# Block-sparse attention and a squared-ReLU MLP on one core: two transposes, one score block and a weight block change places, and the fixed key blocks change slots

## The chip, the cores and the metric

The kernel runs on one core of a Trainium2 chip. Times are device microseconds (us) from one launch. The engines are PE (matmul), ACT, DVE and POOL (elementwise), and SP, which here only issues DMAs; each works through its own queue in order and waits on semaphores of the others.

## The reference

Four batches, eight heads, 768 positions, head size 64; all in float32. Attention is masked by blocks of 32 positions: a query block sees the first and the last key block (the fixed blocks), its own and its two neighbours (the window), and three blocks drawn at random; the first and the last query block see everything. Behind it stands an MLP.

```python
mask = np.abs(blk_i - blk_j) <= window
mask = mask | (blk_i == 0) | (blk_j == 0) | (blk_i == n_blocks - 1) | (blk_j == n_blocks - 1)
for qb in range(n_blocks):
    for kb in sampled_blocks[qb]:
        mask[qb * block:(qb + 1) * block, kb * block:(kb + 1) * block] = True
scores = np.where(mask, scores, -1000000000.0)
...
attn = attn / (np.sum(attn, axis=-1, keepdims=True) + 1e-09)
return np.matmul(attn, v).astype(np.float32)
...
h = np.maximum(x @ w_in, 0.0)        # x: 3072 x 512, w_in: 512 x 2048
return (h * h @ w_out).astype(np.float32)
```

## The kernel before

**Tiles and slots.** The work is cut into 24 tiles of 128 query rows (six per batch), and each tile into two halves of four heads. A query block of 32 rows has eight key slots of 32: in `KG` (keys) and in `V` (values; slots 0 to 3 are the partition quarters of `VA`, slots 4 to 7 those of `VB`). Slots 0 and 1 hold the fixed blocks, 2 to 4 the random ones, 5 to 7 the window. For the first three tiles, which have a `V` each (`V[0]`, `V[1]`, `V[2]`), the fixed blocks of the values come by one small DMA into one query block's place of `V[0]` (`load_static`), and are copied from there to the other places (`copy_static`, L215: `V[0]` and `V[1]` on ACT, `V[2]` on POOL). The random blocks come by one DMA each from SP (`load_sampled`, L339).

**A half's steps** (class `Half`, L379): scores `s` on PE (L427), maxima `m` on DVE (L439), exponentials `p` on ACT (L481), transposes `pt` on PE (L496), copies `pT` (L506 ACT, L508 DVE), values `pv` on PE (L536), normalization into `x` on DVE (L552 to L567). The first and the last query block of a batch go through the class `Whole` (`g`, `pg`, `ptg`, `pvg`).

**The MLP** takes three tiles at a time (a chunk c). `turn` (L902) transposes the three x on PE into PSUM banks `xt`, splits them on ACT into a high part `xh` and on DVE into the rest `xl`; `hidden` (L922) makes 12 matmuls `ph` of 128 hidden columns f, then `r` and `gp` on ACT; `project` (L952) adds into three output banks `po`. For chunk 0, `project` takes `gp` and a plain `WO[f]`, six rows in the trace of PE for its three float32 matmuls.

**The weights** come as 64-bit words `craw` by DMA from POOL. `cut_next` (L863) takes one block of `cuts` at a time through its stages: load, then three calls later two operations on ACT (L833, L835), one call later two on DVE (L844, L845). `cuts` begins with `PRE` blocks of w_in (part 0), then takes a block of w_out (part 1) and one or more of w_in in turn.

```python
    cuts = [(f, 0) for f in range(PRE)]
    for f in range(NF):
        cuts.append((f, 1))
```

So the order before is w_in 0, 1, 2, 3, w_out 0, 1, w_in 4, and so on; the fourth block's ACT operations stand just ahead of the first `xh`. `W` are the cut blocks of w_in, `WO` those of w_out; `wi` is a block of w_in split in two (L889 ACT, L892 POOL).

**What sets the order.** Each engine's queue is in the order in which the code calls it. The first stage steps a `Stream` of the first three tiles' units until they are done (L1061); at counts of `now` it calls `copy_static` and `cut_next` in between. Then chunk 0 of the MLP runs, and after each yielded group of matmuls the stream of the next tiles is stepped once. PSUM tiles named `s`, `pt`, `xt` and `ph` share five banks that go round; a new one waits for the readers of the fifth before it.

Of the kernel before, what the change touches and what calls it, by code (L numbers as in the profile page):

```python
# [23 lines left out]
BLK = 32  # L24
NBLK = S // BLK
NRAND = 3
# [25 lines left out]
LEAD = 2  # L52
PRE = 4
AHEAD = 3
# [20 lines left out]
CUT_0 = (43, 5)  # L75
LOAD_0 = 36
MORE = 1
KEYS_GAP = 4
CUT_1 = 3

FIXED_0 = (7, 14, 24)
LATE = (0, 4)
# [14 lines left out]
def tile_block_sparse_attention_moe(ctx: ExitStack, tc, kd, knd, qd, qgd, vd, vnd, samp, wcat, out):  # L97
# [108 lines left out]
    def load_static(k, u, eng=nc.sync):  # L206
        us = halves(k, u)
        if us is None:
            return
        n = 1 if k == 0 else NJ  # L210
        src = columns(vd[order[k][0], V_STATIC * BLK :], us)
        src = src.unsqueeze(1).broadcast_to([2 * BLK, n, src.shape[-1]])
        eng.dma_start(places(values_of(k)[0], slice(0, 2 * BLK), slice(0, n), us), src)

    def copy_static(k, i, copy):  # L215

        us = slice(i, i + 1)
        src = places(V[0][0], slice(0, 2 * BLK), slice(0, 1), us)
        dst = places(V[k][0], slice(0, 2 * BLK), slice(1 if k == 0 else 0, NJ), us)
        copy(dst, src.broadcast_to(list(dst.shape)))  # L220
# [45 lines left out]
    def copy_keys(b, t, window=nc.gpsimd.tensor_copy):  # L266
# [3 lines left out]
        for us in (slice(0, 1), slice(1, 2)) if t == 0 else (slice(0, 2),):  # L270
# [21 lines left out]
    def load_kg(b, t):  # L292
# [3 lines left out]
        for j in sorted(groups(t)):  # L296
            for r in range(NRAND):
                nc.sync.dma_start(
                    kg[:, j, 2 + r].rearrange("p b c -> p (b c)").unsqueeze(1), k4[:, bass.ds(vals[NRAND * j + r], 1), :]
                )  # L300
        if t < 2:
            for i in range(2):
                src = k4[:, i * (NBLK - 1)].unsqueeze(1)
                dst = kg[:, :, i].rearrange("p j b c -> p j (b c)")
                nc.sync.dma_start(dst, src.broadcast_to(list(dst.shape)))
# [6 lines left out]
    def static_keys(b, t, u, copy):  # L312

        src = st["kn", b, u][:, 0 : NBLK : NBLK - 1].rearrange("p i a c -> p i (a c)").unsqueeze(1)
        dst = st["kg", b, t][:, :, 0:2, 2 * u : 2 * u + 2].rearrange("p j i a c -> p j i (a c)")
        copy(dst, src.broadcast_to(list(dst.shape)))
# [22 lines left out]
    def load_sampled(k, u, eng, on, midway=None):  # L339
# [7 lines left out]
        for j in sorted(groups(t)):  # L347
            if midway and j == NJ // 2:
                load_window(*midway)
            for r in range(NRAND):  # L350
                at = slice(0, BLK) if r == 2 else slice((2 + r) * BLK, (3 + r) * BLK)
                dst = places(VB if r == 2 else VA, at, slice(j, j + 1), us)
                eng.dma_start(dst, v4[:, bass.ds(vals[NRAND * j + r], 1)])  # L353
# [541 lines left out]
    def split_wo(c, f):  # L895
# [4 lines left out]
        wo[c, f] = split(c, WO[f], f"wo{c}_{f}")  # L900

    def turn(c):  # L902

        xh = pool["x"].tile([P, NCC, TOK], F32R, tag="xh", name=f"xh{c}", bufs=1)
        xl = pool["x"].tile([P, NCC, TOK], F32R, tag="xl", name=f"xl{c}", bufs=1)
        for i in range(UC):
            if c * UC >= MOVED:
# [3 lines left out]
            else:  # L911
                x = X.pop(order[c * UC + i])
                pt = bank(f"xt{c}_{i}")
                for cc in range(NCC):
                    nc.tensor.transpose(pt[:, cc * P : (cc + 1) * P], x[:, cc * P : (cc + 1) * P], ident)
            p3 = pt.rearrange("p (c q) -> p c q", c=NCC)
# [109 lines left out]
    warm = one.tile([P, 1], F32, name="warm")  # L1026
    nc.scalar.activation(warm, negative, AF.Exp)
    st["idx"] = indices()
    start = tc.tile_pool(name="start", bufs=1)
    begin = start.__enter__()  # L1030
    for k in range(1, UC):
        V[k] = [begin.tile([P, NJ, 2, HW // 2], F32, name=f"V{k}{c}") for c in range(2)]
    load_static(0, 0)
    load_q(0, 0)
    load_vn(0, 0, nc.gpsimd)
# [6 lines left out]
    load_window(2, 1)  # L1042
    load_sampled(2, 1, nc.sync, SP)
    first = copy_keys(0, 0)
    for _ in groups(0):
        next(first)
    load_vn(0, 1, nc.gpsimd, begin)
    deque(first, 0)
    deque(copy_keys(0, 1), 0)
    deque(copy_keys(0, 2), 0)  # L1050
    cut_next()
    for i in range(2):
        copy_static(2, i, nc.gpsimd.tensor_copy)
    cut_next()
    fixed = [(FIXED_0[k] + i, k, i) for k in range(2) for i in range(2)]
    side = lambda name: ps_o.tile([P, 512], F32, tag="o", name=name)
# [4 lines left out]
    while work.todo or work.running:  # L1061
# [4 lines left out]
        if fixed and now >= fixed[0][0]:  # L1066
            copy_static(*fixed.pop(0)[1:], nc.scalar.copy)
        if now == LOAD_0:
            cut_next()
        if now >= CUT_0[0] and (now - CUT_0[0]) % CUT_0[1] == 0:  # L1070
            cut_next()
# [12 lines left out]
    for c in range(NCH + 1):  # L1084
        work.drain(c, now)
        for _ in moe(c):
# [6 lines left out]
            if c == 0 and now % CUT_1 == 0 and done < len(cuts) + AHEAD + 2:  # L1093
                cut_next()
# [68 lines left out]
```

## Time and profile before

| | |
|---|---|
| timed runs | 730.67, 734.06, 734.63 us; median 734.06 |
| profiled execution | 729.79 us, its span on the core 727.8 us |
| busy, share of the span | PE 705.2 us (97%), DVE 520.6 (72%), POOL 507.6 (70%), ACT 500.0 (69%) |
| mean granted clock of PE | 0.997 |
| chain of work that ended last | PE 90%, DMA 5%, DVE 2% |
| HBM traffic | 100.54 MB read, 6.29 MB written |

PE, DVE, ACT and POOL shares are means over the whole span. The kernel has a first stage of some 48 us, attention alone, and then a long one in which the MLP's matmuls and the next tiles' attention are interleaved on PE. The timed runs are 0.9 to 4.8 us longer than the profiled one.

### The profile page before, as it was taken

Reading aid. Unit: us, or ns where it says so; the run is one execution under the profiler, and the core shown is the slowest. Engines: PE = TensorE matmul, PEld = TensorE weight load, DVE = VectorE, ACT = ScalarE, POOL = GpSimd, SP = SyncE. Lnnn points to the kernel's source line nnn. Section 1 sums busy time; section 2 is a strip of 40 time slices with the busy share of each in tenths; the row PEclk is TensorE's granted clock in tenths of the full one; section 3 lists DMA queues with packets and bytes.
Section 4 is the critical chain, followed back from the end, with each engine's and each line's share of the span. In section 5 each row is a group of like instructions: output and inputs, shape, how many; then the busy total and the mean of one; then the engine's idle time right before and its main releaser. Section 6 shows DMA issues by size and latency. Waiting matters only on the chain.

```text
span 727.8 us, 21584 instructions
## 1 busy us (share of the span) xinstructions
PE 705.2 (97%) x7648; PEld 572.7 (79%) x7648; DVE 520.6 (72%) x1016; ACT 500.0 (69%) x1114; POOL 507.6 (70%) x612
## 2 busy tenths in 40 slices
PE   5878999999999999999999999999999999999997
PEld 2665666668888888878888888887888888889896
DVE  6887777768787777678886876768887676645442
ACT  5678777888866875688877776578877777533222
POOL 6956583238875776768777586667877577769884
PEclk9999999999999999999999999999999999999999
DMA  9987979654535547846445456666455352101001
GB/s 286 243 298 225 323 245 270 172 173 114 146 99 135 167 120 205 203 120 192 119 125 136 113 156 181 178 163 182 136 144 146 106 156 48 36 1 43 1 1 43
DMA packets 96699, 108.25 MB, mean 149 GB/s; under 512 B 13825, under 2 KB 82178, under 8 KB 96594
## 3 DMA queue, kind: packets, MB, share of 16 engines
q1 hardware_dynamic: 90114, 82.51, 41.8%
q0 software_dynamic: 5904, 23.06, 9.6%
q8 instruction: 61, 1.00, 0.6%
q10 hardware_dynamic: 576, 1.31, 0.5%
q14 instruction: 44, 0.36, 0.2%
HBM read 100.54 MB, written 6.29 MB: 147 GB/s over the span
## 4 chain that ended last, share of the span: by engine, by line
PE 90%; DMA 5%; DVE 2%; SPq 1%; ACT 1%; issue 1%; ACTq 0%
PE ph L929 37%; PE po L969 32%; PE po L958 6%; PE s L427 6%; PE pv L521 5%; DMA V<-in_v_dram 3%; PE pv L718 1%; DMA q<-in_q_dram 1%; PE g L641 1%; PE pv L536 1%; SPq L353 1%; PE pt L496 1%; DVE xl L919 1%; ACT xh L918 0%; DVE mg L656 0%
## 5 line engine op out<-in xcount | busy, mean ns | idle before, releaser
L467 ACT ACTIVATE pm<-p 32x256 f32<-32x256 f32 x528 | 219.2, 415 | 23.9 <-DVE p L450 16.3
L929 PE MATMUL ph<-xh,wi 128*128 128x384 f32 x960 | 201.3, 347 | 1.1 <-DVE wi L891 1.1
L929 PEld LDWEIGHTS ph<-xh,wi 128*128 128x128 f32 x960 | 170.6, 188 | 25.0 <-issue 11.3
L892 POOL TENSOR_TENSOR wo<-WO,wo 128x512 fp32r<-128x512 f32 x112 | 144.5, 1290 | 52.1 <-DVE wo L891 51.6
L933 ACT ACTIVATE r<-ph 128x384 f32<-128x384 f32 x128 | 62.8, 491 | 166.4 <-PE ph L929 166.0
L969 PE MATMUL po<-wo,gh 128*128 128x512 f32 x672 | 175.3, 396 | 0.0
L948 POOL TENSOR_TENSOR gl<-gf,gh 128x384 fp32r<-128x384 f32 x112 | 113.7, 1015 | 72.5 <-DVE gf L945 63.4
L945 DVE SCALAR_TENSOR_TENSOR gf<-ph,r 128x384 f32<-128x384 f32 x112 | 61.9, 553 | 124.0 <-ACT r L933 124.0
L969 PEld LDWEIGHTS po<-wo,gh 128*128 128x128 f32 x672 | 123.9, 188 | 26.0 <-issue 4.5
L929 PE MATMUL ph<-xl,wi 128*128 128x384 f32 x480 | 104.0, 338 | 0.0
L892 POOL TENSOR_TENSOR wi<-W,wi 128x512 fp32r<-128x512 f32 x56 | 72.5, 1294 | 38.2 <-DVE wi L891 18.2
L969 PE MATMUL po<-wo,gl 128*128 128x512 f32 x336 | 98.7, 402 | 0.0
L892 POOL TENSOR_TENSOR wi<-W1B,wi 128x512 fp32r<-128x512 f32 x64 | 83.3, 1301 | 20.1 <-ACT wi L889 17.3
L929 PEld LDWEIGHTS ph<-xl,wi 128*128 128x128 f32 x480 | 85.3, 188 | 0.1
L969 PEld LDWEIGHTS po<-wo,gl 128*128 128x128 f32 x336 | 62.1, 189 | 21.5 <-issue 4.3
L891 DVE TENSOR_REDUCE wo<-WO 128x512 fp32r<-128x512 f32 x112 | 74.9, 669 | 0.0
L439 DVE TENSOR_REDUCE m<-s 128x2 f32<-128x512 f32 (+1 forms) x96 | 61.7, 683 | 8.1 <-PE s L427 7.7
L940 ACT ACTIVATE gh<-r 128x384 fp32r<-128x384 f32 x112 | 58.9, 526 | 9.5 <-ACT r L933 0.4
L427 PE MATMUL s<-KG,q 64*32 64x256 f32 x1344 | 50.1, 382 | 0.0
L958 PE MATMUL po<-WO,gp 128*128 128x512 f32 x96 | 46.5, 620 | 2.7 <-DVE WO L845 2.7
L450 DVE TENSOR_TENSOR p<-s,m 128x512 f32<-128x512 f32 (+1 forms) x72 | 46.1, 681 | 0.3
L473 DVE STREAM_TRANSPOSE pT<-pm 128x1024 f32<-128x1024 f32 (+1 forms) x36 | 41.3, 1146 | 0.3 <-ACT pm L467 0.3
(115 smaller groups left out, 804.7 us busy)
## 6 DMA issues: line engine op xcount, KB each, us to landing
craw<-in_w_dram POOLq DMA_DIRECT2D x32, 512.0 KB, 5.8
V<-in_v_dram SPq DMA_DIRECT2D x462, 32.5 KB, 2.6
KG<-in_k_dram SPq DMA_DIRECT2D x189, 64.0 KB, 1.9
V<-in_v_dram SPq DMA_DIRECT2D x26, 390.0 KB, 6.4
KG<-in_k_dram SPq DMA_DIRECT2D x12, 768.0 KB, 6.1
q<-in_q_dram SPq DMA_DIRECT2D x24, 256.0 KB, 3.4
out_dram<-ot SPq DMA_DIRECT2D x22, 256.0 KB, 5.3
V<-in_v_dram SPq DMA_DIRECT2D x14, 292.5 KB, 6.2
```

The costliest lines, as they stand in the source:

```text
L427: nc.tensor.matmul(self.sb[e][g * BLK : (g + 1) * BLK, i * NSLOT : (i + 1) * NSLOT], q[r, j, pr, :], kg[r, j, :, pr, :], start=True, stop= ...
L439: nc.vector.tensor_reduce(m[at, e], self.sb[e][at].rearrange("p (i c) -> p i c", i=2), axis=AX, op=ALU.max)
L467: nc.scalar.activation(p[a * BLK : (a + 1) * BLK, g], x[g * BLK : (g + 1) * BLK, :, a], AF.Exp, scale=SCALE)
L891: nc.vector.tensor_reduce(w[:, 0], src.unsqueeze(2), axis=AX, op=ALU.max)
L892: nc.gpsimd.tensor_tensor(w[:, 1], src, w[:, 0], op=ALU.subtract)
L929: nc.tensor.matmul(ph[:, :TOK], w, x, start=(i == 0), stop=(i == len(steps) - 1))
L933: nc.scalar.activation(r, ph[:, :TOK], AF.Relu)
L940: nc.scalar.activation(gh, r, AF.Square)
L945: nc.vector.scalar_tensor_tensor(gf, ph[:, :TOK], 0.0, r, op0=ALU.max, op1=ALU.mult)
L948: nc.gpsimd.tensor_tensor(gl, gf, gh, op=ALU.subtract)
L958: nc.tensor.matmul(acc[c][u], g[:, u * P : (u + 1) * P], WO[f], start=(f == 0), stop=(f == NF - 1))
L969: nc.tensor.matmul(acc[c][u], g[:, at], w[:, k], start=first, stop=(f == NF - 1 and g is gl))
```

## The change

It does five things.

1. The first two x of chunk 0 are transposed at count 55 of the first stage, ahead of the last `pv` (`TURN_0`, `turn_x`); the third where all three were.
2. `work.step(0)` is called before `turn`, so the fourth tile's scores `s_3_0` stand ahead of the third x.
3. `PRE` is 3: the order of weight blocks becomes w_in 0, 1, 2, w_out 0, w_in 3, w_out 1, w_in 4.
4. The fixed blocks go to slots 1 and 2, the random ones to 0, 3 and 4, for keys and values. `copy_static` copies all 128 partitions for `V[1]` and `V[2]` (the outer slots are written over by the random blocks' DMAs afterwards; DVE clears them once with two memsets, so that what is copied is defined), and one slot of 32 partitions at a time for `V[0]`.
5. `V[1]`'s copies move to the start of ACT's queue, `V[2]`'s copies on POOL from behind the third tile's keys to behind the first half of the first tile's, and the loads of `V[2]`'s random blocks behind them in the code.

```diff
-PRE = 4
+PRE = 3
...
+TURN_0 = 55
...
+FIXED = 1
+RAND = (0, 3, 4)
+
 CUT_1 = 3
-
-FIXED_0 = (7, 14, 24)
+CUT_AT = 0
+
+FIXED_0 = (7, 20)
...
-    def copy_static(k, i, copy):
+    def copy_static(k, i, copy, n=None):
 
         us = slice(i, i + 1)
-        src = places(V[0][0], slice(0, 2 * BLK), slice(0, 1), us)
-        dst = places(V[k][0], slice(0, 2 * BLK), slice(1 if k == 0 else 0, NJ), us)
+        rows = slice(0, P) if n is None else slice((FIXED + n) * BLK, (FIXED + n + 1) * BLK)
+        src = places(V[0][0], rows, slice(0, 1), us)
+        dst = places(V[k][0], rows, slice(1 if k == 0 else 0, NJ), us)
         copy(dst, src.broadcast_to(list(dst.shape)))
...
+    turned_x = {}
+
+    def turn_x(c, i):
+        x = X.pop(order[c * UC + i])
+        pt = bank(f"xt{c}_{i}")
+        for cc in range(NCC):
+            nc.tensor.transpose(pt[:, cc * P : (cc + 1) * P], x[:, cc * P : (cc + 1) * P], ident)
+        return pt
+
     def turn(c):
...
+        first = turned_x if c == 0 else {}
...
-                x = X.pop(order[c * UC + i])
-                pt = bank(f"xt{c}_{i}")
-                for cc in range(NCC):
-                    nc.tensor.transpose(pt[:, cc * P : (cc + 1) * P], x[:, cc * P : (cc + 1) * P], ident)
+                pt = first[i] if i in first else turn_x(c, i)
...
+    for place in (0, NJ - 1):
+        nc.vector.memset(V[0][0][place * BLK : (place + 1) * BLK, 0], 0.0)
     st["idx"] = indices()
...
     load_static(0, 0)
+    for i in range(2):
+        copy_static(1, i, nc.scalar.copy)
...
-    load_sampled(2, 1, nc.sync, SP)
     first = copy_keys(0, 0)
     for _ in groups(0):
         next(first)
     load_vn(0, 1, nc.gpsimd, begin)
+    for i in range(2):
+        copy_static(2, i, nc.gpsimd.tensor_copy)
+    load_sampled(2, 1, nc.sync, SP)
...
-    for i in range(2):
-        copy_static(2, i, nc.gpsimd.tensor_copy)
...
+        if now == TURN_0:
+            turned_x.update({i: turn_x(0, i) for i in range(UC - 1)})
...
+    work.step(0)
     load_vn(1, 0, nc.gpsimd)
```

**Engine PE, end of the first stage.** The queue before, from the last matmuls of the third tile's second half (`pv_2_1`) to the first `ph` and the fourth tile's scores:

```order
L536 MATMUL pv_2_1_1109<-V_125,pT_2_1_1106 32x65 x4
L915 MATMUL xt_0_1177<-ident,x_0_482 128x128 x4
L915 MATMUL xt_1_1184<-ident,x_1_953 128x128 x4
L915 MATMUL xt_2_1191<-ident,x_2_1101 128x128 x4
L929 MATMUL ph_0_1201<-xh_1175,WI 128x384 x4
L427 MATMUL s_3_0_0_1206<-KG_89,q_3_627 32x256
```

The queue of the change, in two pieces (between them stand six more rows of `pv_2_1` and fourteen of `s_3_0`):

```order
L502 MATMUL pt_2_1_1_1087<-ident,p_2_1_1033 128x128 x4
L914 MATMUL xt_0_1113<-ident,x_0_486 128x128 x4
L914 MATMUL xt_1_1118<-ident,x_1_957 128x128 x4
L542 MATMUL pv_2_1_1123<-V_126,pT_2_1_1110 32x65 x4
L542 MATMUL pv_2_1_1123<-V_127,pT_2_1_1110 32x65 x4
```

```order
L433 MATMUL s_3_0_0_1184<-KG_89,q_3_631 32x256
L433 MATMUL s_3_0_1_1185<-KG_89,q_3_631 32x256
L914 MATMUL xt_2_1213<-ident,x_2_1105 128x128 x4
L942 MATMUL ph_0_1223<-xh_1207,WI 128x384 x8
L942 MATMUL ph_0_1223<-xl_1208,WI 128x384 x4
L942 MATMUL ph_1_1260<-xh_1207,wi_1_1220 128x384 x8
```

`xt_0` and `xt_1` now stand ahead of `pv_2_1`; all of `s_3_0`, 16 rows here and 32 matmuls in the trace, stands ahead of `xt_2` and no longer inside `ph_0`.

**Engine ACT, the turn and the first two hidden blocks.** Before, from the fourth weight block's cut (`W_83` is w_in 3) to the second `r`:

```order
L833 ACTIVATE W_83<-craw_0_951 128x512
L835 ACTIVATE craw_0_951<-craw_0_951,below 128x512
L918 CAST xh_1175<-xt_0_1177 128x4x128
...
L936 ACTIVATE gp_0_1239<-r_0_1237 128x384
L833 ACTIVATE WO_91<-craw_1_1036 128x512
L835 ACTIVATE craw_1_1036<-craw_1_1036,below 128x512
L889 CAST wi_2_1247<-W_82 128x512
...
L481 ACTIVATE p_3_0_1231<-s_3_0_0_1206,m_3_0_1228 128x256 x2
L481 ACTIVATE p_3_0_1231<-s_3_0_1_1207,m_3_0_1228 128x256 x2
L933 ACTIVATE r_1_1280<-ph_1_1262 128x384
```

The same place in the change (`WO_91` is w_out 0, `WO_92` w_out 1):

```order
L839 ACTIVATE WO_91<-craw_1_955 128x512
L841 ACTIVATE craw_1_955<-craw_1_955,below 128x512
L931 CAST xh_1207<-xt_0_1113 128x4x128
...
L949 ACTIVATE gp_0_1243<-r_0_1241 128x384
L839 ACTIVATE W_83<-craw_0_1040 128x512
L841 ACTIVATE craw_0_1040<-craw_0_1040,below 128x512
L895 CAST wi_2_1251<-W_82 128x512
L839 ACTIVATE WO_92<-craw_1_1103 128x512
L841 ACTIVATE craw_1_1103<-craw_1_1103,below 128x512
L487 ACTIVATE p_3_0_1231<-s_3_0_0_1184,m_3_0_1228 128x256 x2
```

w_out 0 and w_in 3 have changed places, and one cut instead of two stands between `wi_2` and the exponentials `p_3_0`. SP's queue is the same row for row; it gets two waits, ahead of the first random block of `V[1]` for ACT's copies and ahead of that of `V[2]` for POOL's.

## Rows read from the trace of the kernel before

**Rows 1.** Waits of PE in the first 60 us: us in total, times, longest us.
```profile
PE po L958 <- DVE WO L845: 2.7, 1, 2.7
...
PE ph L929 <- ACT xh L918: 1.2, 1, 1.2
```

**Rows 2.** Waits of PE from 60 us to the end, same columns.
```profile
PE ph L929 <- DVE wi L891: 1.1, 2, 0.6
```

**Rows 3.** Waits of ACT from 56 to 150 us, same columns.
```profile
ACT r L933 <- PE ph L929: 15.5, 12, 1.9
```

**Rows 4.** Timeline of PE: start us, us, instruction, count [idle before <-releaser].
```profile
43.56 0.53 PE L536 MATMUL pv<-V,pT 128*32 128x65 f32 x21 [1.08 <-ACT pT L506]
...
45.18 1.67 PE L915 MATMUL xt<-ident,x 128*128 128x128 f32 x12
48.04 0.98 PE L929 MATMUL ph<-xh,WI 128*128 128x384 f32 x4 [1.19 <-ACT xh L918]
48.95 1.09 PE L427 MATMUL s<-KG,q 64*32 64x256 f32 x32
...
56.48 4.41 PE L958 MATMUL po<-WO,gp 128*128 128x512 f32 x6 [2.73 <-DVE WO L845]
...
64.93 2.84 PE L958 MATMUL po<-WO,gp 128*128 128x512 f32 x6
```

**Rows 5.** Stretches of 1 us: busy PE, PEld, DVE, ACT, POOL; PE clock; DMA; GB/s.
```profile
57.00:58.00 1.00, 1.00 (x3) 0.38 (x2) 1.00 (x2) 1.00 (x4) 0.83 (x2) 0.78 0.92 217
58.00:59.00 1.00, 1.00 (x3) 0.35 (x2) 0.96 (x2) 0.97 (x3) 0.69 (x2) 0.50 1.02 373
...
60.00:61.00 1.00, 1.00 (x4) 0.48 (x2) 0.52 (x1) 1.00 (x3) 0.00 (x0) 0.51 1.03 243
```

**Rows 6.** Timeline of ACT, columns as in group 4.
```profile
9.45 0.20 ACT L669 ACTIVATE mg<-mg 128x2 f32<-128x2 f32 x1 [6.29 <-DVE mg L668]
...
13.85 1.05 ACT L220 COPY V<-V 64x1040 f32<-64x1040 f32 x1
...
45.20 0.68 ACT L833 ACTIVATE W<-craw 128x512 f32<-128x512 f32 x1 [1.74 <-DMA craw<-in_w_dram]
...
46.45 1.53 ACT L918 CAST xh<-xt 128x512 fp32r<-128x512 f32 x3
...
51.69 0.49 ACT L933 ACTIVATE r<-ph 128x384 f32<-128x384 f32 x1 [3.18 <-PE ph L929]
...
52.64 0.66 ACT L833 ACTIVATE WO<-craw 128x512 f32<-128x512 f32 x1
...
53.83 0.61 ACT L889 CAST wi<-W 128x512 fp32r<-128x512 f32 x1
...
56.77 1.55 ACT L481 ACTIVATE p<-s,m 128x256 f32<-128x256 f32 x4
```

**Rows 7.** Timeline of DVE, same columns.
```profile
2.05 0.18 DVE L134 CAST rows<-si 1x72 f32<-1x72 int32 x1 [2.05 <-DMA si<-in_samp_dram]
...
45.93 0.42 DVE L567 TENSOR_TENSOR x<-pv,rec 128x256 f32<-128x256 f32 x1
...
52.25 0.69 DVE L845 SCALAR_TENSOR_TENSOR W<-craw,W 128x512 int32<-128x512 int32 x1
...
54.69 1.65 DVE L845 SCALAR_TENSOR_TENSOR WO<-craw,WO 128x512 int32<-128x512 int32 x1
```

**Rows 8.** Timeline of POOL, same columns.
```profile
12.31 0.61 POOL L316 COPY KG<-KN 128x512 f32<-128x512 f32 x1 [3.07 <-DMA KN<-in_kn_dram]
...
26.56 2.05 POOL L220 COPY V<-V 64x1040 f32<-64x1040 f32 x2
...
54.53 1.26 POOL L892 TENSOR_TENSOR wi<-W,wi 128x512 fp32r<-128x512 f32 x1 [2.94 <-ACT wi L889]
```

**Rows 9.** DMA issues of the first 12 us: count, KB each, us to landing.
```profile
V<-in_v_dram POOLq DMA_DIRECT2D x1, 585.0 KB, 12.4
...
V<-in_v_dram SPq DMA_DIRECT2D x1, 130.0 KB, 5.7
```

More of the change, by code (lines that the diff above doesn't have):

```diff
@@ L212, in load_static @@
         src = src.unsqueeze(1).broadcast_to([2 * BLK, n, src.shape[-1]])
-        eng.dma_start(places(values_of(k)[0], slice(0, 2 * BLK), slice(0, n), us), src)
-    def copy_static(k, i, copy):
+        eng.dma_start(places(values_of(k)[0], slice(FIXED * BLK, (FIXED + 2) * BLK), slice(0, n), us), src)
+    def copy_static(k, i, copy, n=None):
         us = slice(i, i + 1)
-        src = places(V[0][0], slice(0, 2 * BLK), slice(0, 1), us)
-        dst = places(V[k][0], slice(0, 2 * BLK), slice(1 if k == 0 else 0, NJ), us)
+        rows = slice(0, P) if n is None else slice((FIXED + n) * BLK, (FIXED + n + 1) * BLK)
+        src = places(V[0][0], rows, slice(0, 1), us)
+        dst = places(V[k][0], rows, slice(1 if k == 0 else 0, NJ), us)
         copy(dst, src.broadcast_to(list(dst.shape)))
@@ L277, in copy_keys @@
                 for r in range(NRAND):
-                    to = kg[:, j, 2 + r].rearrange("p (u i) s -> p u (i s)", u=2)
+                    to = kg[:, j, RAND[r]].rearrange("p (u i) s -> p u (i s)", u=2)
                     of = KN.rearrange("p u k i s -> p u k (i s)")
@@ L298, in load_kg @@
                 nc.sync.dma_start(
-                    kg[:, j, 2 + r].rearrange("p b c -> p (b c)").unsqueeze(1), k4[:, bass.ds(vals[NRAND * j + r], 1), :]
+                    kg[:, j, RAND[r]].rearrange("p b c -> p (b c)").unsqueeze(1), k4[:, bass.ds(vals[NRAND * j + r], 1), :]
                 )
@@ L303, in load_kg @@
                 src = k4[:, i * (NBLK - 1)].unsqueeze(1)
-                dst = kg[:, :, i].rearrange("p j b c -> p j (b c)")
+                dst = kg[:, :, FIXED + i].rearrange("p j b c -> p j (b c)")
                 nc.sync.dma_start(dst, src.broadcast_to(list(dst.shape)))
@@ L314, in static_keys @@
         src = st["kn", b, u][:, 0 : NBLK : NBLK - 1].rearrange("p i a c -> p i (a c)").unsqueeze(1)
-        dst = st["kg", b, t][:, :, 0:2, 2 * u : 2 * u + 2].rearrange("p j i a c -> p j i (a c)")
+        dst = st["kg", b, t][:, :, FIXED : FIXED + 2, 2 * u : 2 * u + 2].rearrange("p j i a c -> p j i (a c)")
         copy(dst, src.broadcast_to(list(dst.shape)))
@@ L350, in load_sampled @@
             for r in range(NRAND):
-                at = slice(0, BLK) if r == 2 else slice((2 + r) * BLK, (3 + r) * BLK)
-                dst = places(VB if r == 2 else VA, at, slice(j, j + 1), us)
+                half, place = divmod(RAND[r], NJ)
+                dst = places((VA, VB)[half], slice(place * BLK, (place + 1) * BLK), slice(j, j + 1), us)
                 eng.dma_start(dst, v4[:, bass.ds(vals[NRAND * j + r], 1)])
@@ L1051, in tile_block_sparse_attention_moe @@
     cut_next()
-    for i in range(2):
-        copy_static(2, i, nc.gpsimd.tensor_copy)
     cut_next()
-    fixed = [(FIXED_0[k] + i, k, i) for k in range(2) for i in range(2)]
+    fixed = [(FIXED_0[i] + n, i, n) for i in range(2) for n in range(2)]
     side = lambda name: ps_o.tile([P, 512], F32, tag="o", name=name)
@@ L1066, in tile_block_sparse_attention_moe @@
         if fixed and now >= fixed[0][0]:
-            copy_static(*fixed.pop(0)[1:], nc.scalar.copy)
+            _, i, n = fixed.pop(0)
+            copy_static(0, i, nc.scalar.copy, n)
         if now == LOAD_0:
             cut_next()
+        if now == TURN_0:
+            turned_x.update({i: turn_x(0, i) for i in range(UC - 1)})
         if now >= CUT_0[0] and (now - CUT_0[0]) % CUT_0[1] == 0:
@@ L1092, in tile_block_sparse_attention_moe @@
                 f(*at)
-            if c == 0 and now % CUT_1 == 0 and done < len(cuts) + AHEAD + 2:
+            if c == 0 and (now + CUT_AT) % CUT_1 == 0 and done < len(cuts) + AHEAD + 2:
                 cut_next()
```

## The prediction, made before the changed kernel ran

> **What bounds the kernel now.** I read the waits of PE first, in two parts, then PE's timeline where the parts meet, then its clock there, then the other engines' timelines for the same 15 us. From 60 us to the end PE waits 1.1 us in all [rows 2]: the MLP stage is PE's, and an edit changes the time there only if it changes what PE must do or how soon it begins. So the reader should look at what lies before 60 us. The largest waits there are 1.19 us ahead of the first `ph`, for ACT's `xh`, and 2.73 us ahead of the first `po`, for DVE's second operation on w_out 0 [rows 1, 4]. Behind the longer one the granted clock falls: 0.78 in the stretch from 57 to 58 us, then three stretches at 0.50 to 0.51, the lower level of 1.2 GHz (the first and the last are shown) [rows 5]. The same six `po` matmuls take 4.41 us there and 2.84 us two blocks later [rows 4]. What that costs, in time at full clock, is 0.22 + 0.50 + 0.50 + 0.49 = 1.71 us.
>
> **Why w_out 0 is late.** Its two ACT operations stand behind `gp` of the first hidden block and begin at 52.64; DVE's second operation begins at 54.69 and takes 1.65 us where the same operation took 0.69 at 52.25, because it lies beside POOL's subtraction for `wi` from 54.53 to 55.79 [rows 6 to 8]. It ends at 56.34, PE goes on at 56.48. Nothing was late but the place in the queue: ACT had been idle for 3.18 us until 51.69, waiting for PE [rows 6].
>
> **The change, part by part.** I follow PE's own order and ask at each step when PE would come to it and when its input is there.
>
> *The turn.* The first two x, two thirds of 1.67 us, fit into the 1.08 us in which PE waits for `pT` at 42.48 to 43.56; they overrun it by 0.03 us [rows 4]. The fourth tile's scores (1.09 us, of which about 1.0 is PE's own because neighbours overlap) go where PE waits for the third x's normalization and for `xh`, and leave the place inside the first `ph` [rows 4]. That is **1.0 us** off the stretch behind 48.04.
>
> *When the first `ph` can start.* It needs the third `xh`. On one path the third x is normalized at 46.35 [rows 7], its transposes take a third of 1.67 us [rows 4], its `xh` a third of 1.53 us [rows 6]: 46.35 + 0.56 + 0.51 = 47.42. On the other path ACT first does two operations on the fourth weight block, which landed at 45.20 after 1.74 us of waiting [rows 6], and then three `xh` in a row: 47.98, as now. The load for that block is POOL's, and POOL comes to it up to 2.05 us earlier, since `V[2]`'s copies move from 26.56 into a wait of 3.07 us that ended at 12.31 [rows 8]. The gain is 0 to 0.6 us. I take **0.4**, nearer the first path, because half a microsecond of earlier landing is enough for it.
>
> *The wait for w_out 0.* Between 48.04 and 53.75 (56.48 less 2.73) lie the two hidden blocks and the scores; without the scores 4.7 us are left, so PE comes to the first `po` at about 47.6 + 4.7 = 52.3 [rows 4]. w_out 0 takes the place of w_in 3 on DVE, whose second operation ended at 52.94 [rows 7], and that was behind maxima of scores which PE now makes some 3.6 us earlier. So it is there between about 51.2 (maxima straight behind `xl`) and 52.9. What is left of the wait is 0 to 0.6 us; I take 0, and so **2.73 us** off.
>
> *The clock.* With no such wait the reason for the fall is gone. PE's other waits in the rows, of 1.08 and 1.19 us, were followed by no fall. **1.71 us** off.
>
> *What is late next.* `s_3_0` now takes its banks ahead of the third x, so the first of them goes to `ph_2`, five banks on, and `ph_2` must wait for two of the four exponentials `p_3_0`. ACT, behind the end of `ph_0`: `r` and `gp` 0.95 us (51.69 to 52.64), the cut of w_in 3 1.19 us (as 52.64 to 53.83), `wi_2` 0.61, the cut of w_out 1 1.19, two exponentials half of 1.55: 4.7 us [rows 6]. PE, behind the same point: `ph_1` 2.1 us (53.75 less 51.67, where `ph_0` ended and `r` began) and six `po` 2.84: 4.9 us [rows 4]. So ACT is ahead by 0.2 us, on a sum of five items, each uncertain by a tenth. A little later `pv_3_0` waits for ACT's `pT` in the same way: 4.7 us, then the other two exponentials 0.78, `r` and `gp` 0.95, three more cuts 3.57, `wi_3` 0.61, a copy of about 0.6, makes 11.2 us; PE needs 4.9 + `ph_2` 2.1, transposes and scores about 2.0, `po` 2.84 and four of `ph_3` 0.7, makes 12.5. I put down **0.5 us** of new waits, with 0 and 2.0 as bounds (2.0 is one cut and half of the exponentials late).
>
> *Hidden at nothing.* `V[1]`'s copies, 1.05 us each before, leave the busy part of ACT's queue and stand in the 6.29 us ahead of `mg` [rows 6]; a copy of 128 partitions is not in the trace, I take the 64-partition row with as many elements per partition, and twice it as the upper bound. `V[0]`'s four copies stay in the queue, in an early stretch that I leave at no gain. POOL's pair, 2.05 us and 4.1 at most, lies in the 3.07 us wait, and what it overruns it gives back at 26.56 [rows 8]. The memsets, at most 0.69 us each by the nearest DVE row of that size, lie in the 2.05 us in which DVE waits for the indices [rows 7]. SP's two new waits end at about 9 and 11 us, for loads that stand in SP's queue behind the 9 random blocks of `V[0]` and, for `V[2]`, the 12 of `V[1]`; behind them are queued all of `V[1]` and `V[2]`. Slots are the same in number and size, so matmuls, exponentials and packets don't change in any later tile.
>
> **The sum.** 0.4 + 1.0 + 2.73 + 1.71 - 0.5 = 5.3 us; bounds 0 + 1.0 + 2.1 + 0 - 2.0 = 1.1 and 0.6 + 1.09 + 2.73 + 1.71 = 6.1. Against the profiled execution: 729.79 - 5.3 = 724.5 us. That execution is 4.3 us under the median of the timed runs, and nothing tells where they are longer; I carry the difference: 734.06 - 5.3 = **728.8 us**.
>
> **Rivals.**
>
> *The wait moves to ACT* (0.18). ACT's queue becomes the bound between 50 and 62 us: one cut of 1.19 us later than I count, and PE stands at `ph_2` and again at `pv_3_0`. For it: ACT's margin of 0.2 us. Against it: from 56 us on ACT waits 15.5 us for PE and shows no wait for a DMA [rows 3], so it catches up and weights aren't the limit. The gain is 1.5 to 4 us: about 731.
>
> *The clock's 1.71 us aren't gained* (0.12). Either some shorter wait, ahead of the third x or of `ph_2`, brings the fall back, or the timed runs did not all have it before. For it: one execution is profiled, and the timed ones are longer in places I can't see. Against it: the wait just ahead of the fall goes. The gain is 3.6 us: 730.4. The Trainium skill (TensorE: Matmul & The Clock Gate, "What's actually happening") says that the slow state is the default which activity lifts, and that the slow stretch differs from run to run of one kernel; by it this rival would be no surprise. The one profile here shows the fall behind the longest wait of that stage and can't show its spread.
>
> *The start is held up, and the kernel is slower* (0.05). Place: ACT's `V[1]` copies ahead of `mg`. They need the fixed blocks' DMA, which landed 5.7 us after its issue at 1.2 us [rows 9]; 6.9 + 2 x 1.05 = 9.0, and `mg` starts at 9.45 [rows 6]. From a landing at 7.4 us on every microsecond delays `mg` and with it the whole chain of the first stage. It eats the gain at 12.7 us. Were that DMA as slow as the window's on POOL, 12.4 us [rows 9], it would land at 13.6: 6.2 us lost, 734.06 - 5.3 + 6.2 = 735.0; copies of twice the length make it 737. Against it: SP and POOL issue their first DMAs in the same order as before.
>
> *Nothing moves* (0.03). What PE gains it waits away later, for weights or values that come no earlier: 734. Against it stand the small waits of PE and ACT later on [rows 2, 3].
>
> **Chances and range.** The forecast holds 0.62, with its own range of 727 to 730. A measurement of this kernel can tell about 0.5% from no change, 3.7 us. Faster by more: all of the forecast, 0.03 of the first rival, half of the second: 0.71. Within: the rest of these, 0.01 of the third, the fourth: 0.25. Slower: 0.04. For the range I leave out the slow start and the worst of the first rival above, and below take the best sum, 727.9, less some of the 3.4 us by which the fastest timed run lies under the median: 725 to 732.5.
>
> **What would show it.** Right: in the profile of the change, the `xt` of two tiles lie ahead of 43.6 us; `ph` starts between 47.4 and 48.0, one scores block earlier in PE's order; no wait for w_out 0 ahead of `po`, at about 52.3; no stretch at 0.50 between 50 and 65 us; PE's third `po` group of chunk 0 some 5 us earlier than now. Wrong: a wait at `ph_2` or `pv_3_0` over 1 us (ACT), a clock fall anywhere in 45 to 65 us, an `mg` later than 9.5 us, or a stage before 42 us that has grown or shrunk by over 1 us, which I count at nothing.

## The result and the profile after

The changed kernel's first four runs took 724.42, 726.07, 724.64 and 725.66 us, median 725.15, beside 733.48 of four runs of the kernel before: a ratio of 0.9896, 95% interval 0.9868 to 0.9924. The forecast was 728.8 us in a range of 725.0 to 732.5, so the result lies 0.15 us above the range's lower end. The medians are 8.3 us apart, the two profiled spans 5.2 (727.8 and 722.6), the predicted sum was 5.3. Which of these is the change's is what the experiments had to settle. Of all the runs below, four that took over 760 us, in the chip's slow state, are left out.

The page of the changed kernel begins with (span; busy us, share and count of each engine; the granted clock of PE in 40 slices):

```profile
span 722.6 us, 21593 instructions
...
PE 703.0 (97%) x7648; PEld 572.3 (79%) x7648; DVE 522.7 (72%) x1018; ACT 502.8 (70%) x1116; POOL 509.8 (71%) x612
...
PEclk9999999999999999999999999999999999999999
```

PE is busy 2.2 us less than before with the same 7648 matmuls, and the rest of the 5.2 us is waits and pauses. Its waits from 55 us to the end (us in total, times, longest us), as in [rows 1, 2]:

```profile
PE ph L942 <- DVE wi L897: 1.1, 2, 0.6
PE pv L542 <- DMA V<-in_v_dram: 0.9, 1, 0.9
```

The 2.73 us for w_out 0 are gone, and 0.92 us for values is new. PE's timeline, columns as in [rows 4], shows each step of the prediction:

```profile
42.53 1.04 PE L914 MATMUL xt<-ident,x 128*128 128x128 f32 x8
43.49 0.43 PE L542 MATMUL pv<-V,pT 128*32 128x65 f32 x13
44.55 0.99 PE L542 MATMUL pv<-V,pT 128*32 128x65 f32 x51 [0.63 <-issue]
45.47 1.09 PE L433 MATMUL s<-KG,q 64*32 64x256 f32 x32
46.49 0.66 PE L914 MATMUL xt<-ident,x 128*128 128x128 f32 x4
47.82 1.68 PE L942 MATMUL ph<-xh,WI 128*128 128x384 f32 x8 [0.67 <-ACT xh L931]
...
52.16 2.74 PE L971 MATMUL po<-WO,gp 128*128 128x512 f32 x6
54.33 1.26 PE L942 MATMUL ph<-xh,wi 128*128 128x384 f32 x4
...
62.33 1.12 PE L542 MATMUL pv<-V,pT 128*32 128x65 f32 x64
...
64.89 2.74 PE L971 MATMUL po<-WO,gp 128*128 128x512 f32 x6
...
89.25 0.99 PE L542 MATMUL pv<-V,pT 128*32 128x65 f32 x50 [0.92 <-DMA V<-in_v_dram]
```

The eight transposes of the first two x lie at 42.53, ahead of the last `pv` as forecast. The fourth tile's scores stand at 45.47, the third x behind them, and the first `ph` starts at 47.82 after 0.67 us for `xh` in place of 1.19 [rows 4]. The two hidden blocks then run without a gap, and the first `po` is there at 52.16 with no wait; its six matmuls take 2.74 us where they took 4.41 [rows 4]. `ph_2` (54.33) and `pv_3_0` (62.33) don't wait. The third `po` group starts at 64.89; in the trace before it is this row:

```profile
70.97 2.74 PE L958 MATMUL po<-WO,gp 128*128 128x512 f32 x6
```

So 6.08 us are gained there, and 0.92 us of them are waited away at 89.25, since PE now reaches the first half of tile 4 before its values have landed.

The stretches that were at half clock before [rows 5] are at full clock (same columns as there):

```profile
57.00:58.00 1.00, 1.00 (x14) 0.74 (x20) 0.14 (x1) 1.00 (x3) 0.00 (x0) 1.00 1.13 389
...
60.00:61.00 1.00, 1.00 (x3) 0.38 (x2) 0.97 (x3) 1.00 (x3) 0.55 (x2) 1.00 0.85 238
```

ACT's timeline, as in [rows 6]:

```profile
5.91 2.02 ACT L226 COPY V<-V 128x1040 f32<-128x1040 f32 x2 [2.75 <-DMA V<-in_v_dram]
8.83 0.20 ACT L675 ACTIVATE mg<-mg 128x2 f32<-128x2 f32 x1 [0.91 <-DVE mg L674]
...
42.97 0.69 ACT L839 ACTIVATE WO<-craw 128x512 f32<-128x512 f32 x1
43.56 0.77 ACT L841 ACTIVATE craw<-craw,below 128x512 int32<-128x512 uint16 x1
...
47.18 0.58 ACT L931 CAST xh<-xt 128x512 fp32r<-128x512 f32 x1 [0.54 <-PE xt L914]
```

`V[1]`'s two copies start when the fixed blocks have landed, at 5.91, and take 2.02 us for both: one of 128 partitions takes no longer than one of 64 did, 1.05 [rows 6]. They are over 0.9 us before `mg`'s input is there, and `mg` starts at 8.83, earlier than the 9.45 of before. At 42.97 ACT takes the fourth block, now w_out 0, straight behind its other work, with no wait for the load as in [rows 6]; so it is free at 44.3, and the third `xh` waits only for its transposes. DVE and POOL, as in [rows 7, 8]:

```profile
50.52 0.69 DVE L851 SCALAR_TENSOR_TENSOR WO<-craw,WO 128x512 int32<-128x512 int32 x1
...
53.26 1.65 DVE L851 SCALAR_TENSOR_TENSOR W<-craw,W 128x512 int32<-128x512 int32 x1
```

```profile
9.26 2.05 POOL L226 COPY V<-V 128x1040 f32<-128x1040 f32 x2
11.97 0.61 POOL L322 COPY KG<-KN 128x512 f32<-128x512 f32 x1 [0.66 <-DMA KN<-in_kn_dram]
```

w_out 0's last operation on DVE ends at 51.21, 0.95 us before PE asks for it, and takes 0.69 us; the 1.65 us of [rows 7] now falls on a block of w_in (53.26), which nobody waits for. `V[2]`'s copies fill POOL's wait for `KN`, of which 0.66 us are left of the 3.07 in [rows 8].

### The profile page after: what moved, and what is told of

Same layout as the page of the kernel before. It is cut to its first block, busy times and chain, and to the rows that moved or that the text cites. A ratio compares the mean times of both kernels' runs of the same rounds, so it can differ in the third digit from the quotient of the medians.

```text
span 722.6 us, 21593 instructions
## 1 busy us (share of the span) xinstructions
PE 703.0 (97%) x7648; PEld 572.3 (79%) x7648; DVE 522.7 (72%) x1018; ACT 502.8 (70%) x1116; POOL 509.8 (71%) x612
## 4 chain that ended last, share of the span: by engine, by line
PE 89%; DMA 6%; DVE 2%; SPq 1%; ACT 1%; issue 1%; ACTq 0%
PE ph L942 37%; PE po L982 32%; PE s L433 6%; DMA V<-in_v_dram 6%; PE pv L527 5%; PE po L971 5%; PE pv L724 1%; PE g L647 1%; PE pv L542 1%; SPq L359 1%; PE pt L502 1%; DVE xl L932 1%; PE xt L914 0%; SPq L252 0%; DVE mg L662 0%
## 5 line engine op out<-in xcount | busy, mean ns | idle before, releaser
L971 PE MATMUL po<-WO,gp 128*128 128x512 f32 x96 | 44.8, 601 | 0.0
```

What stands on the lines that cost most here:

```text
L971: nc.tensor.matmul(acc[c][u], g[:, u * P : (u + 1) * P], WO[f], start=(f == 0), stop=(f == NF - 1))
```

## Experiments

Twelve experiments ran in three series, each series on one chip beside the kernel before; two of them are the changed kernel again. Besides the time, each run has its span and mean granted clock, so the time that half clock cost a run is (1 - clock) x span; the profile before gives 0.003 x 727.8 = 2.2 us by this, and 1.71 us at 57 to 61 us [rows 5] are the larger part of it (the rest is a fall in the last 1.2 us of the span). "Half clock" is the mean of that over the runs, "without it" the median of the time less it. Both are estimates: the clock is given to 0.001 of the span, 0.7 us; the fall at the end of the span stands behind PE's last matmul in every profile that has it, so it costs nothing, but it counts for 0 to 1.4 us, 0.8 on the mean of the 14 profiles; and the records of the clock begin only 8 to 17 us into the span. Intervals in the text behind a difference of such numbers come from drawing the runs anew.

| kernel | runs | median us | ratio to before, 95% interval | half clock us | without it us |
|---|---|---|---|---|---|
| before, series 1 | 33 | 732.07 | | 3.30 | 728.90 |
| e1_pre3 | 11 | 727.00 | 0.9938 [0.9912, 0.9965] | 1.25 | 726.27 |
| e2_turn | 12 | 730.35 | 0.9975 [0.9946, 1.0004] | 2.31 | 727.90 |
| e3_slots | 12 | 732.27 | 1.0003 [0.9978, 1.0028] | 3.35 | 728.46 |
| e4_pre4 | 12 | 731.59 | 1.0004 [0.9982, 1.0026] | 3.95 | 727.41 |
| before, series 2 | 26 | 731.25 | | 2.19 | 728.95 |
| e5_fill | 12 | 730.91 | 0.9988 [0.9965, 1.0011] | 1.64 | 728.72 |
| e6_again (the change) | 9 | 725.95 | 0.9920 [0.9891, 0.9948] | 1.85 | 724.17 |
| e7_late | 8 | 726.01 | 0.9924 [0.9896, 0.9951] | 1.63 | 724.31 |
| e8_no_slots | 10 | 725.57 | 0.9930 [0.9905, 0.9955] | 1.74 | 724.56 |
| before, series 3 | 24 | 731.08 | | 2.99 | 728.35 |
| e9_pv40 | 9 | 726.05 | 0.9925 [0.9894, 0.9956] | 2.58 | 723.64 |
| e10_pre2 | 12 | 726.06 | 0.9919 [0.9891, 0.9948] | 1.27 | 724.88 |
| e11_load | 6 | 724.12 | 0.9889 [0.9846, 0.9932] | 1.69 | 722.74 |
| e12_change (the change) | 9 | 726.03 | 0.9913 [0.9881, 0.9945] | 1.13 | 724.33 |

### One part of the change at a time: e1, e2, e3, e4

**e1_pre3** is the kernel before with one line of the change.

```diff
-PRE = 4
+PRE = 3
```

> The kernel before with PRE = 3 alone: w_out 0 is cut fourth, nothing else moves. My theory (the wait of PE for w_out 0 and the clock fall behind it are two terms of their own): PE comes to the first po at 53.8 us, finds w_out 0 there, no stretch at half clock follows; 2.7 + 1.7 = 4.4 us faster than before in the profile, all but 1 us of the whole gain. Rival (the wait only moves to ACT's next cuts): a new wait of 1 us or more at ph_2 or pv_3_0, and 2 to 3 us faster. Rival on the timed runs (what they gained over the 5.2 us of the spans, some 2 to 3 us, is clock falls that the timed runs of before had more of): 6 to 7 us faster in the timed runs; if that excess comes from the first stage instead, 4.4.

Its waits of PE from 55 us on:

```profile
PE ph L929 <- DVE wi L891: 1.1, 2, 0.6
PE pv L536 <- ACT pT L506: 0.6, 1, 0.6
```

The wait for w_out 0 is gone, no fall of the clock is left between 15 and 722 us, and the span is 724.0, 3.8 us under the kernel before. Timed, it is 5.1 us faster, of which 2.05 us are half clock and 2.6 us the rest: close to the 1.71 and 2.73 us of the prediction (intervals 1.2 to 2.9 and 2.0 to 3.5). In its place `pv` waits 0.65 us for ACT's `pT`.

**e2_turn** is the kernel before with the other part that moves work on PE, and `PRE` left at 4.

```diff
+TURN_0 = 55
...
+        if now == TURN_0:
+            turned_x.update({i: turn_x(0, i) for i in range(UC - 1)})
...
+    work.step(0)
```

> The kernel before with the early turn of two x and the fourth tile's scores ahead of the third x alone; PRE stays 4, slots and copies stay. My theory: the first ph starts at 48.0 as before, because ACT still waits for the fourth weight block; ph_0 ends 1.0 us earlier, and r, gp and w_out 0 follow it 1.0 us earlier, so the wait for w_out 0 stays at about 2.7 us and the clock falls again: 1.0 us faster. Rival (the wait for w_out 0 swallows it, since its time is set by the weights and DVE, not by ph_0): 0 faster, and the wait grows to 3.7 us.

PE's timeline at the first `ph` and the first `po`:

```profile
49.13 1.68 PE L937 MATMUL ph<-xh,WI 128*128 128x384 f32 x8 [0.68 <-ACT xh L926]
...
56.37 4.42 PE L966 MATMUL po<-WO,gp 128*128 128x512 f32 x6 [2.73 <-DVE WO L846]
```

PE comes earlier to a w_out 0 that is still late: the wait is 2.73 us, as before, and the six matmuls take half-clock time. The whole gain is what was taken out ahead of it, 1.0 us without the half clock (0.3 to 2.1), 1.7 us by medians, where the interval of the ratio just includes none.

**e3_slots** has the new slots, `V` copies and memsets alone, with the old order on PE.

```diff
+FIXED = 1
+RAND = (0, 3, 4)
...
-FIXED_0 = (7, 14, 24)
+FIXED_0 = (7, 20)
...
+    for i in range(2):
+        copy_static(1, i, nc.scalar.copy)
...
-    load_sampled(2, 1, nc.sync, SP)
...
+    for i in range(2):
+        copy_static(2, i, nc.gpsimd.tensor_copy)
+    load_sampled(2, 1, nc.sync, SP)
...
-    for i in range(2):
-        copy_static(2, i, nc.gpsimd.tensor_copy)
```

> The kernel before with the slots, the copies and their places alone; PRE stays 4, no early turn, no early scores. My theory: 0 to 0.6 us faster, through the fourth weight block's load, which POOL issues some 3 us earlier; the wait for w_out 0 and the clock fall stay. Rival (what the timed runs gained over the spans comes from here, by fewer waits of the first stage for values and copies): 2 to 3 us faster in the timed runs. Rival (the slots cost in the later tiles): slower.

No change: 732.27 beside 732.07. Its span, 730.7, is longer than the kernel before's, and the rows show why (PE's two long pauses, the second row with five of its six matmuls, and three 1-us stretches):

```profile
34.96 0.89 PE L542 MATMUL pv<-V,pT 128*32 128x65 f32 x45 [2.47 <-issue]
...
57.86 4.61 PE L971 MATMUL po<-WO,gp 128*128 128x512 f32 x5 [2.74 <-DVE WO L851]
```

```profile
36.00:37.00 1.00, 1.00 (x16) 0.82 (x22) 0.68 (x4) 0.53 (x2) 0.66 (x3) 1.00 0.96 359
...
58.00:59.00 1.00, 1.00 (x2) 0.48 (x3) 0.96 (x3) 1.00 (x4) 0.70 (x2) 0.50 0.48 94
...
62.00:63.00 1.00, 1.00 (x3) 0.34 (x1) 0.97 (x2) 1.00 (x3) 0.62 (x1) 0.50 1.04 327
```

The half clock behind w_out 0's wait lasts from 57.05 to 63.87, 6.83 us, twice as long as in the profile before. In the profiles of e2 and e4 it is 3.41 us again. So the length of that stretch differs from profile to profile, and one can't price it.

**e4_pre4** is the changed kernel with four pre-loaded blocks again.

```diff
-PRE = 3
+PRE = 4
```

> The changed kernel with PRE back at 4, all else as changed. My theory: the wait for w_out 0 of some 2.7 us and the half clock behind it come back: 4.4 us slower than the changed kernel in the profile, 1 to 1.5 us faster than before. Rival (with scores and turn moved, w_out 0 would no longer be late even in fifth place): equal to the changed kernel.

```profile
55.23 4.36 PE L971 MATMUL po<-WO,gp 128*128 128x512 f32 x6 [2.73 <-DVE WO L851]
```

In this row of its timeline the wait is back to the hundredth, with the half clock behind it (56.35 to 59.77), and timed the kernel is within half a microsecond of the kernel before (731.59 and 732.07): half clock costs it 3.95 us. Everything but `PRE` is worth 1.5 us without the half clock (0.6 to 2.4). Timed, 0.5 us of that is left, which is clear neither of none nor of the 1 to 1.5 us that I expected.

### What the clock follows: e5

**e5_fill** is the kernel before with useless matmuls in the place of the wait: it adds work and removes none.

```diff
+FILL = 16
...
+            if f == 0:
+                fill = bank("fill")
+                for i in range(FILL):
+                    nc.tensor.transpose(fill[:, i % NCC * P : (i % NCC + 1) * P], ident, ident)
```

> The kernel before with 16 useless 128x128 transposes of the identity into a spare bank in front of the first output block, about 2.1 us of work where TensorE waited 2.73 us for w_out 0. It adds work and takes none out. Theory (the half clock comes from the wait): the wait shrinks to about 0.6 us and ends at the same moment, the 3.4 to 6.8 us at half clock behind it go, and the profiled run is 1.7 us under the kernel before, the timed median 1.7 to 3.5 us under it, with a narrower spread. Rival (the clock falls there for another reason, such as the loads of that stretch): the fall stays and the time stays within 0.5 us of the kernel before, or grows by a little.

Three rows of PE's timeline and two 1-us stretches:

```profile
35.62 1.52 PE L537 MATMUL pv<-V,pT 128*32 128x65 f32 x45 [2.26 <-issue]
...
56.64 1.91 PE L961 MATMUL fill<-ident 128*128 128x128 f32 x16
59.55 2.81 PE L963 MATMUL po<-WO,gp 128*128 128x512 f32 x6 [1.00 <-DVE WO L846]
```

```profile
36.00:37.00 1.00, 1.00 (x40) 0.90 (x32) 0.00 (x0) 0.00 (x0) 1.00 (x5) 0.50 0.91 197
...
57.00:58.00 1.00, 1.00 (x12) 1.00 (x10) 0.95 (x2) 1.00 (x3) 0.42 (x1) 1.00 0.89 365
```

The 16 transposes take 1.91 us, the wait shrinks to 1.00 us, and no fall follows it: 57 to 58 us is at full clock where the kernel before had 0.78, and the six `po` take 2.81 us. That speaks for PE's idleness as the cause of the fall there, in one execution. The other profiles agree: in the four with the whole wait of 2.73 us (before, e2, e3, e4) a fall stands at this place, in the ten others none. But this execution has a fall of its own, from 35.23 to 38.64, at a pause of 2.26 us in the first stage that the profile calls "issue". Timed, the kernel is 0.3 us under the kernel before and the interval holds both 1.7 us and none: the gain that I expected is neither shown nor excluded. Its time without half clock is the kernel before's (728.72 and 728.95), as it must be, since the wait ends at the same moment; the interval of that difference is -0.8 to 1.1 us.

### The change again, and without the slots: e6, e12, e8

**e6_again** and **e12_change** are the changed kernel without any edit.

> The changed kernel once more, without any edit, beside the others on one chip. Theory (the profiled spans show 5.2 us of work and wait, and the rest of the timed difference is half clock that the kernel before has in most of its timed runs and in a lesser amount in its profiled one): the ratio is again 0.989 to 0.991 (6.5 to 8 us), its runs lie within 3 us of one another, and those of the kernel before within 8 us. Rival (the first four runs were lucky): the ratio is about 0.993, 5.2 us.

> The changed kernel itself again, beside the last three on one chip. Theory: 0.992 of the kernel before (5 to 7 us), of which 4 to 5 us are left when the half clock of each run is taken out by its granted clock. Rival: a gain that is mostly half clock, under 3.5 us left without it.

Ratios of 0.9920 and 0.9913, medians 5.3 and 5.1 us under the kernel before: the 8.3 us of the first comparison, four runs of each, were partly luck, as the rival in e6's expectation had it. Without the half clock 4.8 and 4.0 us are left. The profiled execution of e12 has a span of 725.4, 2.8 us longer than the first, and its timeline and stretches show where:

```profile
36.23 1.27 PE L542 MATMUL pv<-V,pT 128*32 128x65 f32 x45 [2.10 <-issue]
...
51.93 1.68 PE L942 MATMUL ph<-xh,WI 128*128 128x384 f32 x8 [0.68 <-ACT xh L931]
...
56.27 2.74 PE L971 MATMUL po<-WO,gp 128*128 128x512 f32 x6
```

```profile
37.00:38.00 1.00, 1.00 (x19) 0.82 (x12) 0.39 (x3) 0.00 (x0) 0.70 (x3) 0.50 1.00 330
...
57.00:58.00 1.00, 1.00 (x4) 0.40 (x3) 0.97 (x2) 1.00 (x3) 0.80 (x1) 1.00 1.03 408
```

The pause of 2.10 us in `pv` at 34 to 36 us (1.18 us in the first profile) is followed by a fall from 36.55 to 39.97; the first `ph` comes at 51.93 in place of 47.82. At the first `po` nothing has changed: no wait, 2.74 us, full clock. What differs lies in the first stage. e6's profile is alike, with 2.00 us and a fall from 35.69 to 39.10.

A part of it comes before the pause, and the granted clock doesn't show it. The same matmuls near the start, in the first profile of the change and then in e12's:

```profile
9.79 0.93 PE L706 MATMUL ptg<-ident,pg 128*128 128x128 f32 x6 [1.35 <-ACT pg L682]
10.65 1.08 PE L433 MATMUL s<-KG,q 64*32 64x256 f32 x24
```

```profile
10.99 1.51 PE L706 MATMUL ptg<-ident,pg 128*128 128x128 f32 x6 [2.54 <-ACT pg L682]
12.43 1.95 PE L433 MATMUL s<-KG,q 64*32 64x256 f32 x24
```

In e12 they take 1.6 to 1.8 times as long and begin 1.2 us later, behind a longer wait for ACT's `pg`, and PE comes to the pause in `pv` 2.3 us later. Of the 14 profiles only those of the kernel before, the first of the change and e4 have the short `ptg` of 0.93 us; the other eleven have 1.51.

**e8_no_slots** is e2 with `PRE = 3`, that is the change without its slots and copies.

> The kernel before with two parts of the change, the earlier turn of x and scores and the three pre-loaded input blocks in place of four, without the new places of the key blocks and their copies. Theory (the key places and copies are worth nothing): the time of the changed kernel within 0.7 us, so 724.5 to 726 us and the same waits. Rival (the copies also feed the gain, for example by leaving ScalarE earlier): about 727 us, with a wait of 0.5 us or more for ScalarE or VectorE that the changed kernel has not.

Within 0.4 us of the change in the same series, with no wait for w_out 0: the slots and copies are worth nothing that can be measured (the 0.4 us lie well within the spread of such a difference, 1 to 2 us to either side).

### The value wait, one block fewer, and the pause: e7, e9, e10, e11

**e7_late** moves the value matmuls of one half of tile 4 two pieces later, and **e9_pv40** those of the other half, both in the changed kernel:

```diff
+            if u.name == "0_4_1":     # e9: "0_4_0"
+                lag = {**LAG_1, "v0": LAG_1["v0"] + 2}
```

> The changed kernel with one half's value matmuls (tile 4, second half) two pieces later, behind the remaining eight matmuls of the hidden block that they stood inside. Theory (the 0.92 us wait for the V loads at 89.25 us is given back time that the change opened by arriving earlier): the wait is gone, since 1.6 us of other work stands in front of it, the V loads of the next half start 1.6 us later, and the span is 0.9 us under the changed kernel's. Rival (the loads are the bound there): the wait appears at the next value matmuls, and the span stays within 0.3 us.

> The changed kernel with the value matmuls that waited 0.92 us for V (tile 4, first half) two pieces later, behind the other matmuls of their hidden block. Theory (the wait belongs to executions whose first stage ran without a long stall, since it is the V loads that end last there): no wait for V at this place in any execution, and the median is 0.2 to 0.9 us under the changed kernel's of the same job. Rival (the loads are simply waited for at the next half): no difference, with a wait for V or for VectorE of 0.5 us or more behind it.

e7's expectation names the wrong half: the wait at 89.25 is the first half's, so e7 tells nothing of it (726.01, as the change). In e9, three rows of PE's timeline:

```profile
34.84 0.88 PE L542 MATMUL pv<-V,pT 128*32 128x65 f32 x45 [2.11 <-issue]
...
89.65 0.87 PE L942 MATMUL ph<-xl,wi 128*128 128x384 f32 x4
90.45 1.12 PE L542 MATMUL pv<-V,pT 128*32 128x65 f32 x64
```

Here the `pv` at 90.45 lies behind the hidden block and doesn't wait. Timed there is nothing: 726.05 beside 726.03. The profiles suggest why: of the three of the changed kernel only the first, with the short start and the shortest pause at 32 us, has that wait at all; in e6 and e12 PE comes to this `pv` at 91 us or later, when the values are there.

**e10_pre2** has `PRE = 2` in the changed kernel.

> The changed kernel with two pre-loaded input blocks ahead of w_out 0 in place of three. Theory (with three, no wait for w_out 0 is left, so an earlier one is worth nothing): the same time within 0.7 us, if the third input block, one place later now, still comes ahead of its need; if not, a wait of TensorE for wi 2 of up to 2.7 us and the half clock behind it, 3 to 4 us slower. Rival (w_out 0 was still just in time in many executions): 0.5 to 1.5 us faster.

726.06 beside 726.03: with three blocks ahead w_out 0 is in time, and earlier brings nothing that can be measured.

**e11_load** issues the second of the two early weight loads later.

```diff
-    cut_next()
     cut_next()
     fixed = [(FIXED_0[i] + n, i, n) for i in range(2) for n in range(2)]
...
-        if now == LOAD_0:
+        if now in (LOAD_0 - 2, LOAD_0):
             cut_next()
```

> The changed kernel with one of its two early weight loads issued some 8 us later, when the V loads of the first stage are through, so that the DMA engines have 0.5 MB less at 26 to 36 us, where TensorE stands still for 1 to 2.5 us with no wait that the profile can name. Theory (that stall is of loads that the busy DMA engines hold up): the stall at about 33 us is under 1 us, the clock does not fall behind it, and the mean granted clock of the timed runs is at or over 0.999. Rival (the stall has another cause, or the engines are as full without that load): the stall is 1 to 2.5 us as before and the mean clock 0.997 to 0.998; a later w_out 0 may cost up to 2.7 us more.

```profile
34.42 0.89 PE L542 MATMUL pv<-V,pT 128*32 128x65 f32 x45 [1.10 <-issue]
...
48.69 1.50 PE L942 MATMUL ph<-xh,WI 128*128 128x384 f32 x7 [0.68 <-DVE xl L932]
```

The load went out at 30.96 us, 3.7 us later than the 27.26 of e12, less than I had meant. The pause at 33 us is 1.10 us in this one profile, not under 1 us as I expected, the first `ph` starts at 48.69, and the clock doesn't fall there. The six timed runs have a median of 724.1, 1.9 us under the change in the same series and the best of all kernels here, but the ranges overlap (722.69 to 726.27 and 723.91 to 727.17). The mean clock, 0.9977, is what the rival expected, so that the gain comes by the clock is not shown. It beats the kernel before (0.9889); that it beats the change is likely and not settled.

## Why the prediction was right

**The place of the loss** held: w_out 0 was late by its place in the queue. e1 takes the wait away with one number, and e4 puts it back with the same number, at the 2.73 us that it had before.

**The wait for w_out 0, 2.73 us**: 2.6 us without the half clock in e1's timed runs, all of it in the profiles. PE came to the first `po` at 52.16, forecast 52.3, and DVE was through at 51.21, forecast 51.2 to 52.9.

**The turn, 1.0 and 0.4 us**: e2 gives 1.0 us without the half clock, the change against e1 1.4 to 2.2 us (e1 has 2.6 without the half clock, the change 4.0 and 4.8). In the first profile the first `ph` started at 47.82, 0.22 us earlier than [rows 4], inside the forecast's 47.4 to 48.0. That it fell there is partly luck: the profiles of before and after have the same short start, and in e6 and e12 the first `ph` starts at 51.15 and 51.93. It went by the first of the two paths, x to transposes to `xh`, but the last two take 0.66 and 0.58 us there, where I had put thirds of a group, 0.56 and 0.51, with no gap between.

**New waits, -0.5 us**: none at `ph_2` or `pv_3_0`. The forecast had ACT ahead by 0.2 us. In the trace its first two exponentials end at 54.96 and PE's `po` at 54.90, so the two came level, and `ph_2` goes on without a gap. This is the term that was too large: nothing of the 0.5 us was lost here. The wait that did come, 0.92 us for values at 89.25, I had not seen, and it comes only in some executions.

**The clock, 1.71 us**: the place was right (the fall goes with the wait in e1 and comes back with it in e4), the size is less sure. Over 83 runs half clock took 2.86 us of the kernel before (the three series weighted by runs), over 22 runs 1.61 of the changed kernel, some 0.8 us of each being the end of the span that costs nothing: a gain of 1.25 us, with an interval of 0.6 to 1.9 that still holds 1.71; by series it was 0.34 and 1.86. The stretch at half clock can be longer than the 3.41 us of the one profile before (e3: 6.83), and the changed kernel has some too, from pauses in the first stage. That is a part of the second rival: not that the wait's fall stays, but that others come. The Trainium skill (TensorE: Matmul & The Clock Gate, "What's actually happening") says that the slow stretch at a kernel's start differs from run to run of the same kernel. The traces agree: the first `ptg` takes 0.93 us in one profile of the changed kernel and 1.51 in two.

**The sum** was 5.3; series 2 and 3 give 5.3 and 5.1 by medians. It seems that two errors nearly cancel: about 0.5 us too much for the clock, which is not clear of noise, and 0.4 to 1.2 us too little for the rest (3.6 forecast, 4.0 and 4.8 measured; 4.5 over all 83 and 22 runs, with an interval of 4.1 to 5.0). With no new waits the rest would have been 4.1.

**The level, 728.8**, was too high by about 3 us, and that was the step that failed: "nothing tells where they are longer; I carry the difference" of 4.3 us between the profiled execution and the median of three runs. Over 83 runs the median is 731.8, not 734.06: three runs were too few to show what is usual, and 2.3 us of the difference were chance. The other 2.0 lie in the profiled execution, which was a quick one: 21 of the 83 runs took no longer than its 729.79. The traces show where others are longer: in the first stage. e5, whose first stage is the kernel before's own, has the long start and the long pause, and its first `ph` starts at 51.09 in place of 48.04. By the forecast's own signs, a stage before 42 us that is over 1 us longer, e6 and e12 would have counted against it; e5 shows that this comes without the change. That the timed result, 725.15, lies in the range says little of the level: the changed kernel's runs in series 2 and 3 have medians of 725.95 and 726.03.

**The other rivals.** ACT did not become the bound, and nothing was lost to it. The start was not held up: the fixed blocks landed at 5.83 us, well before the 7.4 us from which it would have cost. That the slots and copies are worth nothing that can be measured is shown by e3 and e8.

## What to carry to other kernels

When a weight's preparation is late by its place in a queue and not by any engine's load, find the number that sets the place and move that alone: here one line gave 5.1 us in its series, where the whole change gave 5.3 and 5.1 in two others, and without it the rest gave 0.5 us, not clear of none. Price a pause of TensorE together with the clock that falls behind it, and take that price from the granted clocks of many runs, since one profile shows one draw; compare the first matmuls too, which the granted clock leaves out. A gain of a few microseconds wants two dozen runs of the kernel before: four against four gave 8.3 us where 5 were real.

## What the runs showed of the hardware

From 15 us to PE's last matmul, the granted clock fell at PE's pauses of 2.73 us in four of four profiles (before, e2, e3, e4), and at pauses of 2.0 to 2.5 us in four of six (e5 2.26, e6 2.00, e7 2.19 and e12 2.10; not in e3 2.47 and e9 2.11, where the stretches behind the pause are at 1.00); at none of 1.8 us or less (e4's 1.79 was the longest). The fall came between 0.8 us before PE went on (e3) and 1.1 us after (e4). It lasted 3.41 us in seven profiles and 6.83 us in e3, at 0.50 of full clock, 1.2 GHz.

In all 14 profiles PE paused behind the 19th of the 64 matmuls of one and the same `pv`, at 31.8 to 34.2 us, for 0.60 to 2.47 us, with no wait that the profile can name, in a stretch in which the DMA engines were busy for 0.8 to 1.2 of the time. In three profiles of the changed kernel it was 1.18, 2.00 and 2.10 us. The five profiles without the new slots have 0.60 to 2.26 us, the nine with them 1.10 to 2.47, so whether the slots lengthen it is open.

The traces give a strong hint at what PE waits for there. The page lists a queue "q8 instruction", with 61 packets of 16 KB in each kernel. The pause ends 1.2 to 1.6 us after one of these packets is through, in all 14 profiles, however long the pause is. The same holds for every pause called "issue" between 15 and 60 us, 27 with these 14. This fits a PE that waits for its next instructions. No run changed these packets, so it is not shown as the cause; e11, with one load issued 3.7 us later, had 1.10 us in its single profile.
